# Weights decoded inside their own tile, one scaling of the first output weights, bounds in bfloat16, the next tile's input split in mid-tile, and due times from a backward schedule

## The chip, the cores and the metric

One core of one Trainium2 chip. The metric is the device time of one execution in microseconds (us). Of the core's engines this kernel uses TensorE (PE, matrix products; PEld is its weight load), VectorE (DVE), ScalarE (ACT), SyncE (SP, which here only issues DMA transfers) and, at the start, GpSimd (POOL). Each engine works through its own instructions in the order in which they were issued.

## The reference

```
out_up    = repeat(softmax(q_d k_d^T / 8) v_d, 4)          # q_d, k_d, v_d: means over 4 positions
out_local = softmax(mask(q k^T / 8, |i - j| < 4)) v
x  = (out_up + out_local) as 2304 tokens x 512             # 4 batches x 576, 8 heads x 64
h1 = x @ w1_in       (512 x 2048);  g1 = max(h1, 0) + log1p(exp(-|h1|));  y = g1 @ w1_out  (2048 x 512)
h2 = y @ w2_in       (512 x 2048);  g2 = h2 * cos(h2);                    z = g2 @ w2_out  (2048 x 512)
```

The weights arrive as float64, seen by the kernel as pairs of 32-bit integers, and are turned into float32 on the chip. A float32 product is made of three float16 products: each operand is scaled by a power of two and split into a high and a low float16, and high times high, high times low and low times high are added up in PSUM.

## The kernel before

**Tiles.** The 2304 tokens are four tiles of 512 and one of 256 (tile 4). The 2048 hidden features are 16 blocks f of 128. A unit is one (layer, tile, f): 12 matmuls of 512 columns make h (L884 and L897, PSUM ring h of two slots), ScalarE and VectorE turn it into g, high and low (L905 to L917 in layer 1, L930 to L945 in layer 2, then L966 and L970), and 12 matmuls add g's share to the layer's output (L974 and L989 in layer 1, L1016 and L1031 in layer 2), six for each of two accumulators, called half-units here. The output half lags its input half by LAG = 4 units.

**Weights.** A weight matrix is 8 blocks b of two f, 1 MB each as float64. L440 loads a block into one of two slots stg; ScalarE rebases the upper words into a float tile x (L453, a ring of three), VectorE shifts it (L458, join1, through the helper's L339) and puts in the lower words (L461, join2); ScalarE takes the sum of magnitudes as a bound (L467), and its elementwise output, which nobody reads, goes to the place of the block's final weights. From join2 on stg is free again; x is held until the block's low part is made. The bounds go through a transposing float32 matmul, the spread (L378, into a slot of ring h), and a maximum over columns (L385) to every partition; small VectorE steps make a power of two of it; then come the high part (L497) on ScalarE (L354) or VectorE (L356) and the low part on VectorE (L350). W1I, the first input weights, is scaled block by block; W1O, the first output weights, in four groups of two blocks, each with a scale of its own.

**Stages.** Four pairs of heads of the attention come first (12 more are put between units at fixed steps, POS1 to POS3), then layer 1 on tile 0 while W1I and W1O are decoded, then the other tiles, during which W2I and W2O are decoded, then layer 2. In tile 0 of layer 1 the four groups of W1O close their accumulators after every four f, and L1011 adds groups 1 to 3 to the output in float32. A tile's input must be scaled and split before its first unit: bounds per 128 features, a spread (ident_s by am), then high, low and a copy (L850, L378, L855 with L866 and tile xs). In layer 2 this is written at f = 0 of the tile itself (y_in, L1127); before tile 4 the backlog of output halves is drained to none (drain(0)).

**Order.** Every piece of work is an operation of a plan with a cost for each engine that may take it. `due` walks the operations from the last to the first and gives each the latest time at which it may end; only TensorE is taken there as something that does one thing at a time. `order` then lists the operations by due time, picks the engine where there is a choice, and puts fillers, matmuls of zeros (L1195), where TensorE would wait in the first 350 us of the plan. The order so found is pinned for every engine, and so are the filler matmuls.

## Time and profile before

| | us |
|---|---|
| median of 3 runs | 947.76 (947.12 to 948.87) |
| profiled execution, its own time | 947.95 |
| its span in the profile | 946.2 |
| TensorE busy | 899.2 (95%) |
| VectorE busy | 690.4 (73%) |
| ScalarE busy | 470.0 (50%) |

Busy TensorE is not all needed work: it includes the filler matmuls. The mean granted clock of TensorE was 0.986 of full speed; the two levels are 1.2 and 2.4 GHz, so that 0.50 in a row means the lower of them. In the timelines one row stands for several matmuls in a row on one line; the end of a matmul is modelled, and the distance of starts is the better measure of a unit.

### The profile page before, as it was taken

How to read it: one execution, taken by the hardware profiler on the slowest of the kernel's cores; microseconds unless marked ns; L12 is line 12 of the kernel's file. 1: busy time of each engine (PE TensorE's matmuls, PEld its weight loads, DVE VectorE, ACT ScalarE, POOL GpSimd, SP SyncE). 2: the span in 40 equal slices, each digit the busy share in tenths (PEclk: the TensorE clock that was granted, in tenths of full speed). 3: DMA queues.
4: the chain of work that ended last, by engine and by line, in shares of the span. 5: the costliest groups of instructions: out<-in, count | busy, mean ns of one | idle time of the engine just before them, and what ended most of it. 6: DMA issues, size and time to landing. Idle time of an engine off the chain costs nothing.

```text
span 946.2 us, 14558 instructions
## 1 busy us (share of the span) xinstructions
PE 899.2 (95%) x5809; PEld 469.7 (50%) x5809; DVE 690.4 (73%) x1474; ACT 470.0 (50%) x823; POOL 1.6 (0%) x11
## 2 busy tenths in 40 slices
PE   7899887799999999999999999999999999999797
PEld 4555443345555554444446864444444444444364
DVE  7999999976668776999964566567557656755465
ACT  3464696525445467879866632234224323422243
POOL 0000000000000000000000000000000000000000
PEclk9999998899999999999999999999999999999899
DMA  9557332400122003442200000010001000100100
GB/s 312 164 168 243 119 128 89 171 26 27 31 64 104 1 1 118 152 175 89 90 1 1 1 2 0 1 42 4 1 1 45 1 1 1 45 1 1 44 1 23
DMA packets 13363, 58.89 MB, mean 62 GB/s; under 512 B 1520, under 2 KB 1648, under 8 KB 9200
## 3 DMA queue, kind: packets, MB, share of 16 engines
q1 hardware_dynamic: 13296, 57.97, 17.7%
q8 instruction: 45, 0.74, 0.3%
q14 instruction: 22, 0.18, 0.1%
HBM read 53.25 MB, written 4.72 MB: 61 GB/s over the span
## 4 chain that ended last, share of the span: by engine, by line
PE 74%; DVE 16%; ACT 6%; DMA 2%; issue 1%; SPq 0%; ACTq 0%; DVEq 0%
PE h L897 34%; PE any L1031 19%; PE any L989 17%; DVE td L350 1%; DVE x L461 1%; PE any L724 1%; DVE sm L342 1%; DVE w1i_t L350 1%; DMA vd<-vd 1%; ACT ta L905 1%; DVE xt L350 1%; DMA qk<-qk 1%; DVE rs L602 1%; PE any L675 1%; DVE g L342 1%
## 5 line engine op out<-in xcount | busy, mean ns | idle before, releaser
L897 PE MATMUL h<-xt,w2i_t 128*128 128x512 f16 (+1 forms) x960 | 201.5, 362 | 9.5 <-DVE xt L866 5.3
L897 PE MATMUL h<-xt,w1i_t 128*128 128x512 f16 (+1 forms) x960 | 199.4, 360 | 9.3 <-DVE red L385 6.6
L1031 PE MATMUL any<-w2o_t,g 128*128 128x512 f16 x864 | 197.1, 379 | 0.3 <-DVE g L362 0.3
L989 PE MATMUL any<-g,w1o_t 128*128 128x512 f16 (+1 forms) x864 | 179.5, 357 | 2.3 <-ACT ed L646 1.4
L897 PEld LDWEIGHTS <-w2i_t 128*128 128x128 f16 x960 | 95.3, 99 | 105.7 <-issue 11.5
L897 PEld LDWEIGHTS <-w1i_t 128*128 128x128 f16 x960 | 93.8, 98 | 102.6 <-issue 14.2
L989 PEld LDWEIGHTS <-w1o_t 128*128 128x128 f16 x960 | 93.7, 98 | 89.1 <-issue 4.8
L930 ACT ACTIVATE ta<-h,quarter,i 128x512 f32<-128x512 f32 (+1 forms) x80 | 58.8, 735 | 155.2 <-PE h L897 155.2
L1031 PEld LDWEIGHTS <-g 128*128 128x128 f16 x864 | 84.5, 98 | 100.6 <-DVE g L362 0.8
L342 DVE TENSOR_TENSOR g<-td,g 128x512 f16<-128x512 f32 (+1 forms) x152 | 96.3, 634 | 8.0 <-ACT g L360 1.3
L905 ACT ACTIVATE ta<-h,i 128x512 f32<-128x512 f32 (+1 forms) x80 | 51.4, 642 | 80.7 <-PE h L897 67.4
L935 DVE TENSOR_SCALAR tb<-ta 128x512 f32<-128x512 f32 (+1 forms) x80 | 32.0, 400 | 77.6 <-ACT ta L930 77.1
L945 DVE SCALAR_TENSOR_TENSOR td<-h,r,tc 128x512 f32<-128x512 f32 (+1 forms) x80 | 55.8, 697 | 42.9 <-ACT tc L941 41.2
L941 ACT ACTIVATE tc<-ta 128x512 f32<-128x512 f32 (+1 forms) x80 | 46.9, 586 | 74.5 <-DVE ta L342 74.5
L350 DVE SCALAR_TENSOR_TENSOR td<-ta,sg,tb 128x512 f32<-128x512 f32 (+1 forms) x64 | 43.7, 682 | 48.4 <-ACT ta L917 48.0
L917 ACT ACTIVATE ta<-ta,one 128x512 f32<-128x512 f32 (+1 forms) x80 | 54.2, 680 | 2.0
L362 DVE CAST g<-td 128x512 f16<-128x512 f32 (+1 forms) x124 | 49.4, 398 | 8.0 <-PE any L989 0.8
L342 DVE TENSOR_TENSOR ta<-ta,tb 128x512 f32<-128x512 f32 (+1 forms) x80 | 51.0, 638 | 2.4
L909 ACT ACTIVATE tb<-h,r 128x512 f32<-128x512 f32 (+1 forms) x80 | 51.1, 639 | 0.0
L913 ACT ACTIVATE ta<-ta 128x512 f32<-128x512 f32 (+1 forms) x80 | 46.9, 588 | 0.0
L453 ACT ACTIVATE x<-stg 128x1024 f32<-128x1024 f32 x32 | 36.8, 1149 | 14.1 <-DVE w2i_t L350 3.8
L1195 PE MATMUL h<-zero 128*128 128x512 f16 x133 | 34.4, 393 | 5.3 <-POOL zero L1186 2.4
(147 smaller groups left out, 848.8 us busy)
## 6 DMA issues: line engine op xcount, KB each, us to landing
qk<-qk SPq DMA_DIRECT2D x16, 589.0 KB, 6.6
stg<-w1i SPq DMA_DIRECT2D x8, 1024.0 KB, 7.0
stg<-w1o SPq DMA_DIRECT2D x8, 1024.0 KB, 6.4
stg<-w2i SPq DMA_DIRECT2D x8, 1024.0 KB, 4.8
stg<-w2o SPq DMA_DIRECT2D x8, 1024.0 KB, 4.8
vw<-vw SPq DMA_DIRECT2D x16, 320.0 KB, 4.3
vd<-vd SPq DMA_DIRECT2D x16, 288.0 KB
out<-osb SPq DMA_DIRECT2D x18, 256.0 KB, 2.1
```

The costliest lines, as they stand in the source:

```text
L342: eng[e].tensor_tensor(out=out, in0=in0, in1=in1, op=op)
L350: nc.vector.scalar_tensor_tensor(out=out, in0=raw, scalar=s, in1=other, op0=ALU.mult, op1=op)
L362: nc.vector.tensor_copy(out, in_)
L897: nc.tensor.matmul(h.t[:, 0:n], l, r, start=(i == 0), stop=(i == 11))
L905: act(n, 1, True), lambda: nc.scalar.activation(out=a(), in_=h.t[:, 0:n], func=AF.Abs, scale=col(o.i1, f)),
L909: act(n, 1, True), lambda: nc.scalar.activation(out=b(), in_=h.t[:, 0:n], func=AF.Relu, scale=col(o.r1, f)),
L913: act(n), lambda: nc.scalar.activation(out=a(), in_=a(), func=AF.Exp, scale=-1.0),
L917: act(n, 1), lambda: nc.scalar.activation(out=a(), in_=a(), func=AF.Ln, bias=one),
L930: act(n, 2, True), lambda: nc.scalar.activation(out=a(), in_=h.t[:, 0:n], func=AF.Identity, scale=col(o.i2, f), bias=quarter), [h, *sc], [ ...
L945: dve(n, False, 1), lambda: nc.vector.scalar_tensor_tensor(out=td.t[:, 0:n], in0=h.t[:, 0:n], scalar=col(o.r1, f), in1=r(), op0=ALU.mult, ...
L989: nc.tensor.matmul(a.t[:, i, 0:n], l, r, start=(first and j == 0), stop=(last and j == 2))
L1031: nc.tensor.matmul(a.t[:, i], l, r, start=(f == 0 and j == 0), stop=(f == NF - 1 and j == 2))
```

## The change

- **In place.** A weight matrix is one flat tile of 17 half-blocks of 1024. The floats of block b lie where low(b) and high(b + 1) will stand. The ring x is gone; high(b) can be written only after low(b - 1) was made. The bound's unread output goes into stg, so a slot stg is held until the bound instead of until join2.
- **Groups.** W1I is decoded and scaled in two groups of four blocks. All of W1O is decoded from f = 10 of tile 0 on, its bounds are taken in two groups of four, and one set of steps scales all 16 columns together; layer 1 on tile 0 then has one accumulation over 16 f, as the other tiles have. W2 is scaled by pairs of blocks.
- **bfloat16 bounds.** The bounds of weights and inputs, and the matrix of ones-on-the-diagonal by which they are spread, are bfloat16.
- **Mid-tile.** In layer 2 the next tile's input is written into the plan at f = 8 of the tile before it, and tile 4 starts with four units still in the backlog.
- **Engines fixed.** For the first two batches of heads the copies C0, C1, D1 and up are on ScalarE alone, and so are the high parts of W1, of tile 0's and of tile 1's input, and a small step B1a of the attention.
- **Plan.** `due` schedules backward with VectorE and ScalarE, too, doing one thing at a time. The positions of four head pairs (POS1) and some costs of TensorE operations are changed.

```
 
 LAG = 4
-POS1 = (2, 5, 8, 11)
+POS1 = (6, 10, 15, 20)
 POS2 = (33, 37, 41, 45)
 POS3 = (50, 55, 60, 65)
 LAT = {"pe": 0.2, "act": 0.145, "dve": 0.13, "pool": 0.06, "sp": 0.95}
-NQK, NVD, NVW, NSM, NXB, NST, NGS = 3, 2, 3, 3, 3, 2, 8
+NQK, NVD, NVW, NSM, NST, NGS = 3, 2, 3, 3, 2, 8
-W2STEP = 1
+W2STEP = 2
+W2G = 2
+QKP, VP = (), ()
+YIN = 8
+DR4 = 4
+A_W, A_C, A_X, A_G = True, True, True, False
+CAP = ("pe", "dve", "act")
+OUT0 = 10
+IN0 = ((0, 4), (4, 4))
...
+        pre = {op: [] for op in self.ops}
+        for op in self.ops:
+            for x in op.succ:
+                pre[x].append(op)
...
+        while n:
+            best = None
+            cand = list(ready)
+            if pes and not left[pes[-1]]:
+                cand.append(pes[-1])
+            for op in cand:
+                for e in op.cost:
+                    x = (min(free[e], end[op]) if e in CAP else end[op], op.n)
+                    if best is None or x > best[0]:
+                        best = (x, op, e)
+            (x, _), op, e = best
+            if op is (pes[-1] if pes else None):
+                pes.pop()
+            else:
+                ready.remove(op)
+            op.due = x - op.cost[e]
+            if e in CAP:
+                free[e] = op.due
+            n -= 1
+            for q in pre[op]:
+                end[q] = min(end[q], op.due - LAT[min(q.cost, key=lambda z: q.cost[z])])
+                left[q] -= 1
+                if not left[q] and "pe" not in q.cost:
+                    ready.append(q)
 
         first = {}
         for op in self.ops:
...
 
-                raw, x = STG_.new(), XB_.new()
+                raw, x = STG_.new(), ("float", self.name, b)
...
                 def bound():
-                    nc.scalar.activation(
-                        out=self.t[:, 2 * b : 2 * b + 2, 0, :].bitcast(BF16), in_=x.t, func=AF.Abs,
-                        accum_out=self.bd[:, b : b + 1],
...
+                            out=out.rearrange("p (m e) -> p m e", m=2), in_=self.floats(b), func=AF.Abs,
+                            accum_out=self.bd[:, b : b + 1],
+                        )
+
+                P.add(act(1024), rebase, [raw], [x], [], nm + " rebase")
                 P.add(dve(1024, True), join1, [], [x], name=nm + " join1")
                 P.add(dve(1024), join2, [raw], [x], name=nm + " join2")
-                P.add(act(1024, 1), bound, [x], [("bd", self.name, b), *self.keys(b)], name=nm + " bound")
-                return x
+                P.add(act(1024, 1), bound, [x], [("bd", self.name, b), raw], name=nm + " bound")
...
-            def split(self, b, x):
-                w, s = lambda: self.t[:, 2 * b : 2 * b + 2], self.s[:, 2 * b : 2 * b + 1]
-                k = ("s", self.name, b)
+            def split(self, b):
+                s = self.s[:, 2 * b : 2 * b + 1]
+                x, k = ("float", self.name, b), ("s", self.name, b)
                 nm = f"{self.name}{b}"
+                over = [("float", self.name, b - 1)] if b else []
                 P.add(
-                    {**act(1024, 1), **dve(1024, True, 1)}, lambda e: scaled(e, w()[:, :, 0, :], x.t, s),
-                    [x, k], self.keys(b), name=nm + " high",
+                    either(act(1024, 1), dve(1024, True, 1), self.first and A_W), lambda e: scaled(e, self.his(b), self.floats(b), s),
+                    [x, k], self.keys(b) + over, name=nm + " high",
                 )
                 P.add(
-                    dve(1024, False, 1), lambda: less("dve", w()[:, :, 1, :], x.t, s, w()[:, :, 0, :]),
-                    [x, k], self.keys(b), name=nm + " low",
+                    dve(1024, False, 1), lambda: less("dve", self.los(b), self.floats(b), s, self.his(b)),
+                    [k], self.keys(b) + [x], name=nm + " low",
                 )
 
         W1I, W1O, W2I, W2O = Weight("w1i", w1i), Weight("w1o", w1o), Weight("w2i", w2i), Weight("w2o", w2o)
         W1I.place(wp)
         W1O.place(wp)
-        STG_, XB_ = STG, XB
+        STG_ = STG
+        raw0 = [dp.tile([128, 512], F32, name=f"raw{c}") for c in range(NC_)]
 
 
...
 
-        def group_scale(g):
+        def first_scale():
+
             o = T[0]
-            q = slice(4 * g, 4 * g + 4)
             return [
-                lambda: nc.vector.tensor_tensor(out=gs, in0=bits(o.lc[:, q]), in1=bits(W1O.s[:, q]), op=ALU.add),
-                lambda: nc.vector.tensor_reduce(col(kg, g), gs, axis=AX.X, op=ALU.min),
-                lambda: ts(bits(col(o.ikg, g)), col(kg, g), -1.0, ALU.mult, 381.0 * T23, ALU.add),
-                lambda: ts(bits(W1O.s[:, q]), bits(o.lc[:, q]), -1.0, ALU.mult, col(kg, g), ALU.add),
+                lambda: nc.vector.tensor_tensor(out=gs, in0=bits(o.lc), in1=bits(W1O.s), op=ALU.add),
+                lambda: nc.vector.tensor_reduce(o.k, gs, axis=AX.X, op=ALU.min),
+                lambda: ts(bits(o.ik), o.k, -1.0, ALU.mult, 381.0 * T23, ALU.add),
+                lambda: ts(bits(W1O.s), bits(o.lc), -1.0, ALU.mult, o.k, ALU.add),
             ]
 
...
-        def grp_in(b):
-            x = W1I.decode(b)
-            then = in_scale(0, 2 * b, 2, W1I, 14) + relu_scale(0, 2 * b, 2, T[0].lc)
-            W1I.scale(b, 1, then, [("sx", 0)], [("sc0", b)])
-            W1I.split(b, x)
-
-        def grp_out(g):
-            xs = [W1O.decode(2 * g), W1O.decode(2 * g + 1)]
+        def grp_in(b, n):
+            for i in range(n):
+                W1I.decode(b + i)
+            W1I.scale(b, n)
+            for i in range(n):
+                W1I.split(b + i)
+            then = in_scale(0, 2 * b, 2 * n, W1I, 14) + relu_scale(0, 2 * b, 2 * n, T[0].lc)
+            steps(
+                then, [("s", "w1i", b + i) for i in range(n)] + [("sx", 0), ("c", 0)],
+                [("sc0", b + i) for i in range(n)], "wthen",
+            )
+
+        def grp_out():
+            for b in range(NB):
+                W1O.decode(b)
+            W1O.scale(0, 4)
+            first = [("sc0", b) for b in range(NB)]
             W1O.scale(
-                2 * g, 2, group_scale(g), [("sc0", 2 * g), ("sc0", 2 * g + 1)],
-                [("sc0g", g)] + [("s", "w1o", 2 * g), ("s", "w1o", 2 * g + 1)],
+                4, 4, first_scale(), first + [("s", "w1o", b) for b in range(4)],
+                [("sc", 0)] + [("s", "w1o", b) for b in range(NB)],
             )
...
         for f in range(NF):
-            if f % 2 == 0:
-                grp_in(f // 2)
+            if f // 2 in dict(IN0) and f % 2 == 0:
+                grp_in(f // 2, dict(IN0)[f // 2])
+            if f == OUT0:
+                grp_out()
             unit_in(1, 0, f)
             step()
-        for g in range(4):
-            grp_out(g)
         for f in range(NF):
             l2(0, f)
             step()
...
             for _ in range(min(n, len(todo))):
                 W, b = todo.pop(0)
-                x = W.decode(b, after=[P.wrote["place2"]])
-                W.scale(b, 1)
-                W.split(b, x)
+                W.decode(b, after=[P.wrote["place2"]])
+                if b % W2G == W2G - 1:
+                    W.scale(b - W2G + 1, W2G)
+                    for a in range(b - W2G + 1, b + 1):
+                        W.split(a)
 
         for i, (k, t, f) in enumerate(seq):
             if f == 0:
...
         for i, (k, t, f) in enumerate(seq2):
-            if f == 0:
-                if t == 4:
-                    drain(0)
+            if i == 0:
                 y_in(t)
+            if f == YIN and t < 4:
+                y_in(t + 1)
+            if t == 4 and f == 0:
+                drain(DR4)
```

Three places in the order of instructions, first VectorE where the first output weights (w1o) get their scale. s_w1o holds the scales, lc those of the relu, gs, kg and ikg (now gs, k_0 and ik_0) the steps between; td, ta, tb and xt2 or xt3 belong to tile 0's activations, xt1 and xs0 to the input of tile 1, and x0 and x2 are slots of the ring x. Before, a group of two blocks (4 columns):

```order
L385 TENSOR_REDUCE red_1795<-h0_90 128x2
L350 SCALAR_TENSOR_TENSOR td0_96<-ta0_92,lc_0_159,tb0_94 128x512
L339 TENSOR_SCALAR s_w1o_150<-red_1795 128x4
L362 CAST xt2_84<-td0_96 128x512
L339 TENSOR_SCALAR s_w1o_150<-s_w1o_150 128x4
L342 TENSOR_TENSOR xt2_84<-td0_96,xt2_84 128x512
L810 TENSOR_TENSOR gs_219<-lc_0_159,s_w1o_150 128x4
L350 SCALAR_TENSOR_TENSOR td0_96<-ta1_93,lc_0_159,tb1_95 128x512
L811 TENSOR_REDUCE kg_218<-gs_219 128x1
L350 SCALAR_TENSOR_TENSOR xt1_83<-xt1_83,sx_1_179,xs0_97 128x512
L339 TENSOR_SCALAR ikg_217<-kg_218 128x1
L342 TENSOR_TENSOR xt2_84<-td0_96,xt2_84 128x512
L339 TENSOR_SCALAR s_w1o_150<-lc_0_159,kg_218 128x4
L866 COPY xt1_83<-xs0_97 128x512
L356 TENSOR_SCALAR w1o_t_156<-x0_106,s_w1o_150 128x2x512
L356 TENSOR_SCALAR xs0_97<-xt1_83,sx_1_179 128x512
L350 SCALAR_TENSOR_TENSOR w1o_t_156<-x0_106,s_w1o_150,w1o_t_156 128x2x512
L350 SCALAR_TENSOR_TENSOR w1o_t_156<-x2_108,s_w1o_150,w1o_t_156 128x2x512
```

Now, all 16 columns:

```order
L896 TENSOR_TENSOR gs_218<-lc_0_160,s_w1o_147 128x16
L391 SCALAR_TENSOR_TENSOR td0_96<-ta1_93,lc_0_160,tb1_95 128x512
L897 TENSOR_REDUCE k_0_166<-gs_218 128x1
L403 CAST xt3_85<-td0_96 128x512
L380 TENSOR_SCALAR ik_0_167<-k_0_166 128x1
L383 TENSOR_TENSOR xt3_85<-td0_96,xt3_85 128x512
L380 TENSOR_SCALAR s_w1o_147<-lc_0_160,k_0_166 128x16
L391 SCALAR_TENSOR_TENSOR td0_96<-ta0_92,lc_0_160,tb0_94 128x512
L919 TENSOR_REDUCE am1_1_236<-xm_1_181 128x1
L383 TENSOR_TENSOR qt0_116<-qk2_110 128x288 x2
L403 CAST xt3_85<-td0_96 128x512
L391 SCALAR_TENSOR_TENSOR w1o_t_153<-w1o_t_153,s_w1o_147 128x1024
L383 TENSOR_TENSOR xt3_85<-td0_96,xt3_85 128x512
L383 TENSOR_TENSOR qd0_117<-qt0_116 64x144 x2
L383 TENSOR_TENSOR qd0_117<-qt0_116 128x144
L391 SCALAR_TENSOR_TENSOR td0_96<-ta1_93,lc_0_160,tb1_95 128x512
L391 SCALAR_TENSOR_TENSOR w1o_t_153<-w1o_t_153,s_w1o_147 128x1024
```

The steps of four groups became one set; high parts (L356 before) no longer stand on VectorE, and between one low part (L391 STT on w1o_t) and the next other work was put.

Second, ScalarE during the decoding of w1o: the rebase is L453 before and L508 now, the bound L467 and L524. Before:

```order
L917 ACTIVATE ta1_93<-ta1_93,one_80 128x512
L453 ACTIVATE x0_106<-stg1_110 128x1024
L453 ACTIVATE x1_107<-stg0_109 128x1024
L467 ACTIVATE w1o_t_156,bd_w1o_149<-x0_106 128x2x512
L467 ACTIVATE w1o_t_156,bd_w1o_149<-x1_107 128x2x512
L905 ACTIVATE ta0_92<-h0_90,i1_0_157 128x512
L909 ACTIVATE tb0_94<-h0_90,r1_0_161 128x512
```

Now:

```order
L508 ACTIVATE w1o_t_153<-stg0_106 128x1024
L401 ACTIVATE aTd0_128<-any2_89 72x576
L999 ACTIVATE ta0_92<-ta0_92 128x512
L685 ACTIVATE sm1_123<-sm1_123 128x640
L728 ACTIVATE nd_2_229<-nd_2_229 96x3
L1003 ACTIVATE ta0_92<-ta0_92,one_80 128x512
L508 ACTIVATE w1o_t_153<-stg1_107 128x1024
L991 ACTIVATE ta1_93<-h1_91,i1_0_158 128x512
L995 ACTIVATE tb1_95<-h1_91,r1_0_162 128x512
L524 ACTIVATE stg0_106,bd_w1o_146<-w1o_t_153 128x1024
L401 ACTIVATE up0_129<-any0_87 128x144
L734 ACTIVATE ed0_125,sd_2_233<-any1_88,nd_2_229 96x144 x3
L524 ACTIVATE stg1_107,bd_w1o_146<-w1o_t_153 128x1024
```

The rebase of the second slot now stands ahead of the bound of the first, and the bound writes stg.

Third, TensorE where layer 2 goes from tile 3 to tile 4; am2_4 is tile 4's bound, xt4 its input, g the hidden activations. Before (the six last rows of the drain's matmuls, the spread, the first unit):

```order
L1031 LDWEIGHTS g7_105
L1031 MATMUL any1_88<-w2o_t_3386,g7_105 128x512
L1031 LDWEIGHTS g7_105
L1031 MATMUL any1_88<-w2o_t_3386,g7_105 128x512
L1031 LDWEIGHTS g7_105
L1031 MATMUL any1_88<-w2o_t_3386,g7_105 128x512
L378 MATMUL h1_91<-ident_s_77,am2_4_245 128x128
L897 LDWEIGHTS w2i_t_3385
L897 MATMUL h0_90<-xt4_86,w2i_t_3385 128x256
```

Now:

```order
L1109 MATMUL any1_88<-w2o_t_3252,g3_101 128x512
L1109 LDWEIGHTS g3_101
L1109 MATMUL any1_88<-w2o_t_3252,g3_101 128x512
L1109 LDWEIGHTS g3_101
L1109 MATMUL any1_88<-w2o_t_3252,g3_101 128x512
L419 LDWEIGHTS am2_4_244
L419 MATMUL h1_91<-ident_s_77,am2_4_244 128x128
L1109 LDWEIGHTS g4_102
L1109 MATMUL any2_89<-w2o_t_3252,g4_102 128x512
```

The spread of tile 4 moved from the end of tile 3's last output half to a place between two output halves.

## Rows read from the trace of the kernel before

**Rows 1.** The page: span, then busy time of each engine (share, instructions).
```profile
span 946.2 us, 14558 instructions
PE 899.2 (95%) x5809; PEld 469.7 (50%) x5809; DVE 690.4 (73%) x1474; ACT 470.0 (50%) x823; POOL 1.6 (0%) x11
```
**Rows 2.** Stretches: start:end, length, busy us (instructions) per engine, PEclk, DMA share, GB/s.
```profile
0.00:172.00 172.00, 143.83 (x1498) 83.24 (x1499) 162.50 (x383) 104.72 (x205) 1.64 (x11) 0.97 0.51 169
172.00:218.00 46.00, 43.96 (x202) 19.99 (x201) 35.41 (x76) 16.39 (x25) 0.00 (x0) 0.95 0.27 98
218.00:887.00 669.00, 663.88 (x3819) 336.22 (x3818) 457.42 (x918) 328.25 (x550) 0.00 (x0) 1.00 0.10 35
887.00:905.00 18.00, 11.25 (x55) 6.96 (x54) 10.44 (x36) 5.67 (x12) 0.00 (x0) 0.72 0.16 59
```
**Rows 3.** Timeline of TensorE in layer 2: start, us, line, shapes, count, [idle <- releaser].
```profile
588.73 2.75 PE L897 MATMUL h<-xt,w2i_t 128*128 128x512 f16 x12
591.32 2.75 PE L1031 MATMUL any<-w2o_t,g 128*128 128x512 f16 x12
```
**Rows 4.** Timeline of TensorE where tile 4 of layer 2 begins.
```profile
887.89 0.39 PE L378 MATMUL h<-ident_s,am 128*128 128x128 f32 x2
891.53 0.49 PE L897 MATMUL h<-xt,w2i_t 128*128 128x256 f16 x3 [3.25 <-DVE xt L866]
...
900.29 2.72 PE L897 MATMUL h<-xt,w2i_t 128*128 128x256 f16 x12 [1.48 <-DVE td L945]
902.80 1.74 PE L1031 MATMUL any<-w2o_t,g 128*128 128x512 f16 x6
904.38 2.85 PE L897 MATMUL h<-xt,w2i_t 128*128 128x256 f16 x24
```
**Rows 5.** Timeline of TensorE where tile 1 of layer 2 begins.
```profile
641.83 5.34 PE L897 MATMUL h<-xt,w2i_t 128*128 128x512 f16 x24 [0.92 <-DVE td L945]
```
**Rows 6.** Timeline of TensorE at tile 1 of layer 1.
```profile
218.40 2.75 PE L897 MATMUL h<-xt,w1i_t 128*128 128x512 f16 x12
```
**Rows 7.** Uses of tile xs up to 218: ns min/median/max, first and last start.
```profile
L866 DVE COPY xt<-xs x4: 285/287/289, 152.6 to 171.3; 128x512 f16<-128x512 f16 x4
```
**Rows 8.** VectorE by line and shape, 0 to 200: busy us, mean ns, idle before.
```profile
L461 DVE SCALAR_TENSOR_TENSOR x<-stg,x 128x1024 int32<-128x1024 int32 x16 | 19.3, 1214 | 0.0
...
L339 DVE TENSOR_SCALAR x<-x 128x1024 int32<-128x1024 int32 x16 | 10.9, 685 | 1.2 <-ACT x L453 1.2
...
L350 DVE SCALAR_TENSOR_TENSOR w1i_t<-x,s_w1i,w1i_t 128x1024 f16<-128x1024 f32 x8 | 10.2, 1279 | 0.1
```
**Rows 9.** ScalarE by line and shape, 0 to 200.
```profile
L453 ACT ACTIVATE x<-stg 128x1024 f32<-128x1024 f32 x16 | 18.3, 1143 | 9.6 <-DVE w1o_t L350 3.8 <-DMA stg<-w1i 3.7 <-DVE w1i_t L350 2.0
...
L917 ACT ACTIVATE ta<-ta,one 128x512 f32<-128x512 f32 x16 | 11.5, 726 | 0.2
...
L467 ACT ACTIVATE w1o_t<-x 128x1024 bf16<-128x1024 f32 x7 | 7.4, 1053 | 3.9 <-DVE x L461 3.9
L354 ACT ACTIVATE w1i_t<-x,s_w1i 128x1024 f16<-128x1024 f32 x5 | 5.8, 1155 | 1.0 <-DVE s_w1i L339 1.0
```
**Rows 10.** Stretch 0 to 40, columns as in rows 2.
```profile
0.00:40.00 40.00, 32.15 (x394) 19.37 (x394) 33.44 (x85) 14.48 (x35) 1.64 (x11) 1.00 0.81 273
```
**Rows 11.** The page's DMA issues: KB each, median us to landing.
```profile
stg<-w1i SPq DMA_DIRECT2D x8, 1024.0 KB, 7.0
```
**Rows 12.** Timeline of SyncE's queue, issues of weight blocks.
```profile
75.11 0.33 SPq L440 DMA_DIRECT2D stg<-w1i  x1
...
85.14 0.33 SPq L440 DMA_DIRECT2D stg<-w1i  x1
```
**Rows 13.** Timeline of TensorE around the first output weights.
```profile
148.33 9.94 PE L897 MATMUL h<-xt,w1i_t 128*128 128x512 f16 x36 [5.00 <-DVE red L385]
```
**Rows 14.** Stretch in which those matmuls began, columns as in rows 2.
```profile
146.00:152.00 6.00, 3.67 (x9) 1.32 (x9) 6.00 (x15) 4.30 (x9) 0.00 (x0) 0.50 0.94 350
```
**Rows 15.** TensorE by line and shape, whole program: filler matmuls on ring h.
```profile
L1195 PE MATMUL h<-zero 128*128 128x512 f16 x133 | 34.4, 393 | 5.3 <-POOL zero L1186 2.4 <-ACT tb L909 1.6 <-ACT ed L646 1.1
```

More of the change, by code (lines that the diff above doesn't have):

```diff
@@ L172, in cool @@
                 return False
+            cost = min(cost, 2.4)
             a0 = now + cost - WIN
@@ L554, in sum4, with sums, place @@
                 two(e, vs.t, tv.t[:, :, 0], tv.t[:, :, 1], ALU.add)
-            aop({"dve": 0.74}, sum1, [tk], [qt], [qt, qd], nm + "sum1")
-            aop({"dve": 0.66}, sum2, [qt], [qd], [], nm + "sum2")
+            pa, sm = BANK.new(), SM.new()
+            if b in QKP:
+                hs = (HB if b == 0 else BANK).new()
+                hst = lambda: hs.t if b == 0 else hs.t[:, 0]
+                def sums():
+                    x = tk.t[:, :, 3 : 3 + S].rearrange("p a (i r) -> p a i r", r=4)
+                    for a in range(2):
+                        for r in range(4):
+                            nc.tensor.matmul(
+                                hst()[:, SD * a : SD * a + SD], ident, x[:, a, :, r], start=(r == 0), stop=(r == 3)
+                            )
+                def place():
+                    for j in range(2):
+                        h = slice(64 * j, 64 * j + 64)
+                        copy("act", qd.t[h, SD * j : SD * j + SD], hst()[h, 0:SD])
+                    nc.scalar.activation(
+                        out=qd.t[:, 2 * SD : 3 * SD], in_=hst()[:, SD : 2 * SD], func=AF.Copy, scale=float(2.0**-7)
+                    )
+                aop(pe(2.3), sums, [tk, "ident"], [hs], [hs], "sums " + nm)
+                aop({"act": 0.85}, place, [hs], [qd], [qd], nm + "place")
+            else:
+                aop({"dve": 0.74}, sum1, [tk], [qt], [qt, qd], nm + "sum1")
+                aop({"dve": 0.66}, sum2, [qt], [qd], [], nm + "sum2")
+            nmx, r = carr_small("nm", NG * 2), carr_small("rs", NG * 2)
             if b == 0:
```

171 lines of the change are left out of this document (87 added, 84 removed).

## Prediction

> **What bounds the kernel now.** I read the page first: TensorE is busy for 899.2 of 946.2 us [rows 1], so no other engine can bound the program as a whole, and time is lost where TensorE waits or multiplies zeros. The stretches show where that is. From 218 to 887 it is busy for 663.9 of 669 us at full clock [rows 2]; the change can take little there. Two places remain. From 0 to 172 TensorE is busy for 143.8 us, fillers among it (133 of them on ring h alone [rows 15]), and VectorE for 162.5 of 172 [rows 2]: that first stage belongs to VectorE. From 887 to 905 TensorE is busy for 11.3 of 18 us at 0.72 of its clock [rows 2]: that is the start of tile 4 in layer 2. So I make two sums, A for layer 2 and B for the first stage.
>
> **A, the next tile's input in mid-tile.** The price of TensorE's work: 12 matmuls of 512 columns take 2.59 us from start to start, 588.73 to 591.32 [rows 3], so 0.216 for one, 0.108 for one of 256 columns, and 1.295 for a half-unit of six. Where tile 4 begins, the spread ends at 888.28 and steady work starts at 904.38. Between them lie 36 matmuls of 256 columns and 6 of 512, worth 5.2 us. The other 10.9 us are waiting for the input's split (3.25 at first) and for the first unit's activations (1.48), and the low clock [rows 4, 2]. At tile 1 only 0.92 us is lost [rows 5], for four output halves in the backlog cover the rest; I count that three times, 2.7 in all. In the new order the spread of tile 4 stands between two output halves of tile 3, and the split has half a tile of TensorE's time, over 40 us, to be done in: both losses go, -13.6.
>
> What the move costs: the spread takes a slot of ring h in mid-tile, four times, so that two units in a row share the other slot. Nothing in the trace shows that. It is bounded by zero, for the output halves may cover it, and by the 0.92 of [rows 5], a wait for the same chain of activations. I take about the middle, 0.5 each, +2.0. The splits' VectorE work is moved, not added, and VectorE has 211 us to spare between 218 and 887 [rows 2]. **A = -11.6.**
>
> **B, the first stage.** My landmark is the first matmul of layer 1 on tile 1. It stands at 218.40 now [rows 6], although its input's last copy started at 171.3 [rows 7]: after that TensorE had the output matmuls of tile 0 to do, 43.96 of 46 us [rows 2]. In the new order it stands in the middle of these matmuls, and waits for that same copy. So I ask when VectorE gets there, and how much of TensorE's work is then left.
>
> VectorE's work up to that copy, counted in the two orders. More: three blocks more to join (16 for 13) at 1.21 + 0.69, so +5.7, and six low parts more (16 for 10) at 1.28, +7.7 [rows 8]. Less: attention steps (177 for 206 instructions), high parts and input high parts (none for 9), small steps (38 for 58) and reductions (6 for 11). The 63 that go are worth, at 0.2 to 0.4 us each (VectorE's mean here is 162.5 us over 383, 0.42 [rows 2], and short steps pull it down), 13 to 25 us. So VectorE's work is the same or up to 12 us less; I take the same, 162.5 us, since most of what goes is short. The four groups' extra additions of L1011 lie behind the copy and no longer matter.
>
> VectorE's idle time was 9.5 us of 172 [rows 2], of which 6.6 at the very start [rows 10], while the first loads land; that stays. New are two waits. One is the staging: a slot now takes a landing of 7.0 [rows 11], a rebase of 1.14, joins of 0.69 and 1.21 and a bound of 1.05 [rows 8, 9], 11.1 us at least, and two slots serve 16 blocks in 8 rounds. The issues at 75.11 and 85.14, one slot's turn with the other slot's issue between them, are 10 us apart [rows 12], so such rounds occur. The first issue is at some 10 us and the last bound must be done at about 138 for the rest of the order to fit behind it, so there are 16 us for a round, and queue waits of up to 4.9 fit in. I let VectorE stand for 1.1 us a round, 9 in all; the bounds are 1.2, the idle time that the rebase ends now [rows 8], and 39 if all 4.9 fell on it. The other is the chain in W1O: each high part, 1.16 on ScalarE [rows 9], waits for the low part before it, and each low part for its high part. Ahead of a high part may stand an activation of 0.73 [rows 9], so up to 1.9 for each of eight blocks, 15 us; the order has other VectorE work between two low parts, so at least 0. I take 3.5, nearer to zero for that reason. Idle time 6.6 + 9 + 3.5 = 19, and the copy is done at 162.5 + 19 = 181.5.
>
> TensorE at that point: by the order 15 of the 32 half-units of tile 0's output stand behind the landmark, 19.4 us that lay ahead of it before; a few small products of the attention more and cheaper spreads are about even. The 17 ahead of it, 22 us, need the first low part of W1O at about 159, which is where VectorE's sum stands there.
>
> The clock: after a wait of 5.00 us, 36 matmuls took 9.94 us, and 7.77 by the steady price [rows 13]; the granted clock was 0.50, the lower level, in that stretch [rows 14]. The output of tile 0 now starts after one longer wait for W1O, so +2.2. **B** = 181.5 + 19.4 + 2.2 - 218.4 = **-15.3**.
>
> Of the other parts: scaling W2 by pairs and decoding it in place lies beside a TensorE that is 99% busy [rows 2], at zero; if that cover failed it would show as waits of the first units of layer 2 for w2i, at most one round, 11 us. The new due times have no price of their own; what they do is in the order that I counted from.
>
> The Trainium skill ("SBUF — State Buffer", section "The DMA setup-cost knee") says that a transfer of 1 MiB lands at about 330 to 340 GB/s, an estimate of 3.1 us for a block. By that the rounds would be almost 4 us shorter, the staging stalls would vanish and the time would be about 912. Here other loads run beside them, the trace has 7.0 us [rows 11], and the measurement decides.
>
> **Sum.** 946.2 - 11.6 - 15.3 = 919.3 of span; the profiled execution took 947.95, 1.75 more than its span, and 0.2 more than the median of the runs, which I leave out. So 921.
>
> **Rivals.**
> 1. Staging turns against it, slower. The slot is held through the bound, and in ScalarE's order the next slot's rebase stands ahead of that bound, so a late join blocks both slots. Every microsecond on a round moves the landmark by 8. The gain of 26.9 is gone at 3.4 us more, a round of 19.4; at 20.5 the time is 921 + 36 = 957. For it: the ring of three x that decoupled the joins is gone, and ScalarE already sat 9.6 us ahead of the rebases [rows 9]. Against it: at 16 the round has 4.9 us over its parts.
> 2. The first stage gains nothing: high and low parts take turns at full price (+11.5) and staging takes some 4 us more. A alone is left: 936.
> 3. The split in mid-tile doesn't do what it says, because VectorE comes to it only late in the tile; A is zero: 932.6. Against it: VectorE is busy for 457 of 669 us there [rows 2].
> 4. The clock. There are 140 filler matmuls for 205. If each of some five waits of the first stage that had fillers now ends at the lower level, at 2.2 each [rows 13], the time is 932. The Trainium skill ("TensorE: Matmul & The Clock Gate", section "What's actually happening") speaks for it: the default state is throttled, and activity releases it. The trace agrees as far as [rows 14] goes. Against it: the fillers are placed in the new plan by the same rule, and the mean clock was 0.97 up to 172 [rows 2].
>
> **How the numbers follow.** Chances: forecast 0.56, rival 2 0.20, rival 1 0.12, rival 4 0.07, rival 3 0.05. The range: with idle time as before (9.5 less), no clock cost and no cost in ring h it would be 907; at the top it takes in rivals 2 to 4. So 906 to 938; above it lies rival 1, and parts of the others. What measurement can tell from no change here is about 0.2%, 1.9 us. Faster by more than that are the forecast and rivals 2 to 4 nearly whole, 0.87; rival 1 gives 0.10 to slower and, with the thin end of rival 2, 0.03 to no difference.
>
> **What would show it.** The first matmul of layer 1 on tile 1 at about 200 or before, within 4 us of the end of VectorE's copy of tile 1's input, with 15 half-units behind it; VectorE's idle time up to there near 19 us; slot rounds of 16 us by the issues of weight blocks; and at the start of tile 4 no wait of TensorE over 1 us and a granted clock of 1.00. I would be wrong if TensorE waits for W1O beyond 165, if VectorE's waits for ScalarE's rebases come to over 30 us, or if waits in layer 2 at ring h exceed 1 us per tile.

## The result and the profile after

The changed kernel took 903.11 us (median of 4 runs, 901.8 to 904.3) against 947.81 in the same batch: a ratio of 0.9527, 95% interval 0.9511 to 0.9544. That is 44.7 us less where 26.9 were forecast, and lies below the range of 906 to 938. The direction was right and the two places were right; the sizes were too small. The profiled execution has a span of 900.0 us, 46.2 less than before; it was the fastest of its four (901.8), so spans and landmarks that are compared with it below mostly show 1 to 2 us more than the medians do.

The page of the changed kernel, first the lines that answer to [rows 1]:

```profile
span 900.0 us, 14222 instructions
PE 869.6 (97%) x5702; PEld 452.8 (50%) x5702; DVE 659.1 (73%) x1352; ACT 480.4 (53%) x861; POOL 1.6 (0%) x11
...
PEclk9999999999999999999999999999999999999999
```

The granted clock no longer has a slice under 0.9. Stretches, columns as in [rows 2]:

```profile
0.00:170.40 170.40, 145.55 (x1462) 81.24 (x1462) 161.26 (x332) 126.66 (x240) 1.64 (x11) 0.99 0.55 187
140.00:172.00 32.00, 29.20 (x136) 13.04 (x134) 31.83 (x63) 21.39 (x30) 0.00 (x0) 1.00 0.14 43
600.00:860.00 260.00, 260.00 (x1249) 121.94 (x1248) 166.41 (x332) 86.28 (x132) 0.00 (x0) 1.00 0.04 13
```

170.40 is the landmark of the prediction, the first matmul of layer 1 on tile 1 (218.40 before, [rows 6]). Up to it VectorE works for 161.3 us, 1.2 less than in the 172 us of [rows 2], and is idle for 9.1. From 600 to 860 in layer 2 TensorE does not wait at all. The same in the timelines of TensorE, first around the landmark (L1074 is the output half of layer 1, L983 the input half, L419 a spread):

```profile
145.92 2.75 PE L1074 MATMUL any<-g,w1o_t 128*128 128x512 f16 x12
148.67 0.22 PE L419 MATMUL h<-ident_s,am 128*128 128x128 bf16 x1
148.73 7.93 PE L1074 MATMUL any<-g,w1o_t 128*128 128x512 f16 x36
156.49 10.52 PE L1074 MATMUL any<-xt,w1o_t 128*128 128x512 f16 x48
169.11 1.46 PE L1074 MATMUL any<-g,w1o_t 128*128 128x512 f16 x6 [2.09 <-DVE sm L383]
170.40 2.75 PE L983 MATMUL h<-xt,w1i_t 128*128 128x512 f16 x12
```

The outputs of tile 0 begin at 145.92 and run at full clock; 102 matmuls, 17 half-units, stand ahead of the landmark as counted. TensorE's only wait among them, 2.09 us, ends with a step of the attention on VectorE (sm, which reads a slot of the ring any); the landmark itself follows without a wait. Before, TensorE had fillers and waits from 159 on, and the outputs began at 173.70:

```profile
159.68 5.99 PE L1195 MATMUL h<-zero 128*128 128x512 f16 x27 [0.96 <-ACT tb L909]
...
171.49 0.79 PE L378 MATMUL h<-ident_s,bd_w1o 128*128 128x128 f32 x2 [5.61 <-ACT w1o_t L467]
173.70 14.46 PE L989 MATMUL any<-g,w1o_t 128*128 128x512 f16 x60 [1.42 <-ACT ed L646]
```

Then at the start of tile 4, which answers to [rows 4]:

```profile
840.64 2.75 PE L1109 MATMUL any<-w2o_t,g 128*128 128x512 f16 x12
843.24 2.78 PE L983 MATMUL h<-xt,w2i_t 128*128 128x256 f16 x24
845.86 2.75 PE L1109 MATMUL any<-w2o_t,g 128*128 128x512 f16 x12
```

No idle time, every distance is the steady 2.6 us. What VectorE waited for up to the landmark (us in all, times, longest):

```profile
DVE qt L383 <- DMA qk<-qk: 3.9, 1, 3.9
DVE w1i_t L391 <- ACT w1i_t L395: 1.2, 2, 0.6
DVE w1o_t L380 <- ACT w1o_t L508: 0.9, 1, 0.9
```

The third row is the staging (join1 waits for a rebase): 0.9 us where I had put 9. The second is the chain of high and low parts in W1I, 1.2; in W1O, where I had put 3.5, it is 0.2. The loads, issues on SyncE's queue by start:

```profile
39.26 1.60 SPq L495 DMA_DIRECT2D stg<-w1i  x2
...
50.33 3.81 SPq L495 DMA_DIRECT2D stg<-w1i  x2
...
61.36 6.06 SPq L495 DMA_DIRECT2D stg<-w1i  x2
...
75.35 2.69 SPq L495 DMA_DIRECT2D stg<-w1o  x2
...
86.59 0.33 SPq L495 DMA_DIRECT2D stg<-w1o  x1
...
90.59 0.33 SPq L495 DMA_DIRECT2D stg<-w1o  x1
...
101.17 2.62 SPq L495 DMA_DIRECT2D stg<-w1o  x2
...
113.62 3.66 SPq L495 DMA_DIRECT2D stg<-w1o  x2
```

After a first round of 27.5 us the rounds take 11.0 to 14.6, not the 16 of the forecast. The landings on the page (KB each, median us), for [rows 11]:

```profile
stg<-w1i SPq DMA_DIRECT2D x8, 1024.0 KB, 6.0
stg<-w1o SPq DMA_DIRECT2D x8, 1024.0 KB, 5.0
```

### The profile page after: what moved, and what is told of

The parts are those of the page before. It is cut to its first block, busy times and chain, and to the rows that moved or that the text cites. A ratio compares the mean times of both kernels' runs of the same rounds, so it can differ in the third digit from the quotient of the medians.

```text
span 900.0 us, 14222 instructions
## 1 busy us (share of the span) xinstructions
PE 869.6 (97%) x5702; PEld 452.8 (50%) x5702; DVE 659.1 (73%) x1352; ACT 480.4 (53%) x861; POOL 1.6 (0%) x11
## 4 chain that ended last, share of the span: by engine, by line
PE 75%; DVE 13%; ACT 7%; DMA 3%; issue 1%; SPq 0%; DVEq 0%; ACTq 0%
PE h L983 35%; PE any L1109 21%; PE any L1074 16%; ACT stg L524 1%; DVE sm L383 1%; DMA stg<-w2o 1%; PE any L815 1%; DVE w1o_t L391 1%; DVE td L391 1%; ACT ta L991 1%; DMA stg<-w1o 1%; DVE nm L679 1%; DVE qd L383 1%; ACT tb L995 1%; PE any L716 1%
## 5 line engine op out<-in xcount | busy, mean ns | idle before, releaser
L983 PE MATMUL h<-xt,w1i_t 128*128 128x512 f16 (+1 forms) x960 | 199.5, 360 | 7.5 <-ACT tb L995 3.5
L983 PE MATMUL h<-xt,w2i_t 128*128 128x512 f16 (+1 forms) x960 | 199.0, 358 | 0.0
L1074 PE MATMUL any<-g,w1o_t 128*128 128x512 f16 (+1 forms) x864 | 177.9, 355 | 2.3 <-DVE sm L383 2.1
L983 PEld LDWEIGHTS <-w1i_t 128*128 128x128 f16 x960 | 93.4, 98 | 101.0 <-issue 8.1
L983 PEld LDWEIGHTS <-w2i_t 128*128 128x128 f16 x960 | 93.9, 98 | 94.9
L1074 PEld LDWEIGHTS <-w1o_t 128*128 128x128 f16 x960 | 92.8, 98 | 88.8 <-issue 3.6
L391 DVE SCALAR_TENSOR_TENSOR td<-ta,sg,tb 128x512 f32<-128x512 f32 (+1 forms) x64 | 43.6, 681 | 49.4 <-ACT ta L1003 48.9
L1285 PE MATMUL h<-zero 128*128 128x512 f16 x105 | 27.7, 397 | 3.4 <-POOL zero L1276 2.4
L395 ACT ACTIVATE xs<-xt,sx 128x512 f16<-128x512 f32 (+1 forms) x27 | 18.3, 679 | 20.7 <-DVE xt L952 14.4
```

What stands on the lines that cost most here:

```text
L391: nc.vector.scalar_tensor_tensor(out=out, in0=raw, scalar=s, in1=other, op0=ALU.mult, op1=op)
L983: nc.tensor.matmul(h.t[:, 0:n], l, r, start=(i == 0), stop=(i == 11))
L1074: nc.tensor.matmul(a.t[:, i, 0:n], l, r, start=(first and j == 0), stop=(last and j == 2))
```

## The experiments

Fifteen runs, each beside the kernel before on the same chip; the ratio is to that, with its 95% interval (the changed kernel has 0.9527). "Landmark" is the first matmul of layer 1 on tile 1. Three kinds: parts undone, with a new order by the planner; the same order with one cost changed; one part alone in the kernel before.

| run | median us | ratio | landmark |
|---|---|---|---|
| W1O in four groups again | 928.4 | 0.9771 (0.9724 to 0.9819) | 218.1 |
| input split at the tile's start again | 919.9 | 0.9704 (0.9682 to 0.9727) | 175.8 |
| W1O written at f = 15 | 915.0 | 0.9641 (0.9626 to 0.9655) | 171.5 |
| the same, W1I block by block | 923.4 | 0.9733 (0.9717 to 0.9750) | 206.5 |
| engines free | 908.7 | 0.9581 (0.9563 to 0.9599) | 198.7 |
| due times of before | 905.1 | 0.9548 (0.9517 to 0.9579) | 174.8 |
| slot free from join2, planned so | 914.7 | 0.9638 (0.9601 to 0.9674) | 199.4 |
| same order: float32 bounds | 906.7 | 0.9568 (0.9541 to 0.9594) | 172.4 |
| same order: bound's output elsewhere | 900.3 | 0.9487 (0.9467 to 0.9508) | 169.4 |
| same order: no fillers | 905.2 | 0.9548 (0.9516 to 0.9580) | 175.6 |
| same order: 480 KB more per block | 908.9 | 0.9585 (0.9541 to 0.9630) | 178.6 |
| same order: bound taken twice | 918.3 | 0.9668 (0.9647 to 0.9690) | 187.8 |
| same order: every load twice | 970.7 | 1.0244 (1.0214 to 1.0274) | 241.6 |
| before: split in mid-tile alone | 934.4 | 0.9862 (0.9834 to 0.9890) | 218.7 |
| before: new due times alone | 950.0 | 1.0008 (0.9988 to 1.0027) | 219.1 |

A landmark that moves need not move the end, since a plan may do more of tile 0's outputs ahead of it (engines free: 198.7, but only 5.6 us more). Only between runs of the same order it stands for time. What the parts undone cost is not to be added up either, since each got an order of its own. No run undoes the decoding in place, the pairs of W2's blocks or the new positions of the attention; what these are worth alone is not shown.

**Layer 2.** The split put back to the tile's start:

```diff
-            if i == 0:
-                y_in(t)
-            if f == YIN and t < 4:
-                y_in(t + 1)
-            if t == 4 and f == 0:
-                drain(DR4)
+            if f == 0:
+                if t == 4:
+                    drain(0)
+                y_in(t)
```

> The changed kernel (903.1 us) with one part undone: in layer 2 the next tile's input is written at f = 0 of the tile itself again, and tile 4 starts with an empty backlog. Theory: the input split at the tile's start costs what the kernel before lost there, 10.9 us at tile 4 and 0.9 at each of tiles 1 to 3, so 13.6 more: 916.7, with TensorE waiting for xt at tile 4 and a granted clock under 0.8 there. Forecast's own sum: 11.6 more, 914.7. Rival, that the extra gain lies in layer 2: more than 17 us more, over 920.

919.9, 16.8 more. The loss at tile 4 is back, in rows that copy [rows 4]:

```profile
866.79 0.49 PE L983 MATMUL h<-xt,w2i_t 128*128 128x256 f16 x3 [3.42 <-DVE xt L952]
...
875.57 2.72 PE L983 MATMUL h<-xt,w2i_t 128*128 128x256 f16 x12 [1.48 <-DVE td L1031]
```

That is above the 13.6 expected. The profiled execution has a span 21.2 us longer: from the first unit of layer 2 to the end it takes 394.3 us for 379.5, 14.8 more, and the rest lies ahead, where the first unit of tile 0 starts 6 us later in the new order (64.2 for 58.4). The reverse, in the kernel before:

```diff
-            if f == 0:
-                if t == 4:
-                    drain(0)
+            if i == 0:
                 y_in(t)
+            if f == 8 and t < 4:
+                y_in(t + 1)
+            if t == 4 and f == 0:
+                drain(4)
```

> The kernel before with one part alone: the next tile's input of layer 2 at f = 8 of the tile before, tile 4 started with four units in the backlog. Theory 1: all of the loss at the tiles' starts goes, 13.6 or a little more: 933 to 934.5, no wait of TensorE over 0.5 us in layer 2. Forecast: 11.6 less, 936, with waits of about 0.5 us in mid-tile for ring h. Rival 3: no gain, 947.

934.4, 13.9 less (1.38%, interval 1.10 to 1.66%). Theory 1 holds; at tile 4 TensorE goes through without a wait:

```profile
872.15 2.75 PE L1031 MATMUL any<-w2o_t,g 128*128 128x512 f16 x12
874.74 2.78 PE L897 MATMUL h<-xt,w2i_t 128*128 128x256 f16 x24
```

From the first unit of layer 2 to the end this run takes 389.3 us for 404.2. So A is 13.9 by the medians and 14.9 by the profile, and not 11.6: nothing is paid for the slot of ring h in mid-tile, and the waits that go were 1.3 more than the 13.6 that I had counted.

**The output weights.** W1O in four groups of two blocks, with their accumulators and additions, as the functions of before have it:

```diff
-            if f == OUT0:
-                grp_out()
+            if f == OUT0:
+                for g in range(4):
+                    grp_out(g)
```

> The changed kernel with W1O in four groups of two blocks again, each with its scale, its accumulators and its additions of L1011 (emitted at f = 10 as now). Theory 1: scaling all at once saves VectorE the three further sets of steps and six additions of 1.28 us, about 10 us of work on the engine that sets the first stage, half of it ahead of tile 1's input: 907 to 913. Theory 2: a first group ready early lets TensorE begin the outputs of tile 0 sooner, which is worth as much: 900 to 904.

928.4, 25.3 more, two and a half times what theory 1 allowed; theory 2 falls, as the outputs of tile 0 begin at 156.27 instead of 145.92. VectorE's additions (L1099) account for much of the size, columns as in the other timelines:

```profile
183.22 2.58 DVE L1099 SCALAR_TENSOR_TENSOR xt<-any,ikg,xt 128x1024 f32<-128x1024 f32 x2 [5.16 <-PE any L1077]
193.58 2.58 DVE L1099 SCALAR_TENSOR_TENSOR xt<-any,ikg,xt 128x1024 f32<-128x1024 f32 x2 [7.78 <-PE any L1077]
203.94 1.28 DVE L1099 SCALAR_TENSOR_TENSOR xt<-any,ikg,xt 128x1024 f32<-128x1024 f32 x1 [7.78 <-PE any L1077]
```

The order puts tile 1's last copies behind these additions (they start at 210.1 to 217.1), so VectorE stands for 20.7 us while TensorE works off the groups, and then, from 206 to 218, TensorE has little but fillers and waits. Of the parts undone this one costs most. When W1O is written into the plan matters too:

```diff
-OUT0 = 10
+OUT0 = 15
```

> The changed kernel with W1O written into the plan at f = 15 of tile 0 instead of f = 10 (control for the next run). The order goes by due times, so little is expected: 901 to 907.

915.0, 11.9 more, outside what was expected. The landmark is nearly where it was, but the outputs of tile 0 start late, and TensorE fills the gap:

```profile
150.42 4.69 PE L1285 MATMUL h<-zero 128*128 128x512 f16 x21 [1.30 <-ACT tb L995]
159.52 12.17 PE L1074 MATMUL any<-g,w1o_t 128*128 128x512 f16 x42 [4.41 <-DVE sm L383]
```

42 matmuls took 12.17 us there, the lower clock in the first of them (granted 0.50 from 159.5 to 165); the changed kernel began its outputs at 145.92. So 7 half-units stand ahead of the landmark and not 17, and the other ten, 13 us of TensorE's work, are left for later, which fits the 11.9.

**The input weights,** block by block, on top of the last:

```diff
-IN0 = ((0, 4), (4, 4))
+IN0 = tuple((b, 1) for b in range(8))
```

> As the control, with W1I scaled block by block again (eight sets of steps instead of two). Theory 1: six sets of some eight short VectorE steps more, 6 x 8 x 0.17 = 8 us on the engine that sets the first stage: 6 to 9 more than the control. Theory 2: the first units of tile 0 begin earlier, which pays for the steps: within 3 of the control.

8.4 us over its control, the size of theory 1, but not its mechanism: VectorE's work in the whole program is 663.1 us for 660.9, 2.2 more and not 8. The outputs of tile 0 begin 9.2 us later (168.74 for 159.52), in another order. What causes that is open:

```profile
162.36 3.18 PE L1285 MATMUL h<-zero 128*128 128x512 f16 x14 [0.49 <-DVE red L426]
168.74 6.61 PE L1074 MATMUL any<-g,w1o_t 128*128 128x512 f16 x23 [3.20 <-ACT ed L734]
```

**Engines and due times.**

```diff
-A_W, A_C, A_X, A_G = True, True, True, False
+A_W, A_C, A_X, A_G = False, False, False, False
```

> The changed kernel with the choice of engine given back to the planner (attention copies C0, C1, D1, up, high parts of W1 and of the inputs of tiles 0 and 1). Theory 1: fixing them to ScalarE took about 6 us of work from VectorE, which sets the first stage: 5 to 8 us more, 908 to 911, VectorE busy for 165 us or more up to tile 1's input. Theory 2: the planner chose ScalarE for most of them anyway: 902 to 905.

908.7, 5.6 more: theory 1, and VectorE's work in the whole program is 665.6 us for 659.1, 6.5 more. The due times of before in the changed kernel, and the new ones in the kernel before (the core of the first; the second is its reverse):

```diff
-            op.due = x - op.cost[e]
-            if e in CAP:
-                free[e] = op.due
+            if "pe" in op.cost:
+                end = min(end, nxt)
+                nxt = end - cost
+            op.due = end - cost
```

> The changed kernel with the due times of the kernel before (only TensorE does one thing at a time in them); the parts and their operations are the same, the order is not. Theory 1: the backward schedule with capacities is what keeps VectorE supplied in the first stage; without it VectorE's idle time up to tile 1's input rises from 9 to 19 us or more, the first matmul of layer 1 on tile 1 moves from 170 to over 180, and the time is over 913. Theory 2: the grouping of the weights does it, and the due times matter little: 901 to 907, landmark at 168 to 174.

> The kernel before with the backward schedule with capacities alone (everything else as it was). Theory 1: the due times gave little in the changed kernel (2 us), so also here: 943 to 948. Theory 2: the old order is where the first stage lost its time, TensorE idle from 140 to 172: 920 to 938.

905.1 and 950.0; the first interval overlaps that of the changed kernel, and the second holds 1. So theory 2 of the first run holds (its landmark, 174.8, is just outside what was written), and of the second theory 1 in substance (its time is 2 us above what was written). No gain of the backward schedule can be told here, in either kernel.

**Bounds.** float32 for the six tiles of bounds and ident_s, same order.

```diff
-        ident_s = const.tile([128, 128], BF16, name="ident_s")
+        ident_s = const.tile([128, 128], F32, name="ident_s")
```

> The changed kernel, same order, with the bounds and the spread's matrix in float32 again. Behind the first matmul of tile 1 stand 24 spreads (16 for the second layer's weights, 8 for inputs). Theory 1: a float32 spread costs TensorE some 0.2 us more than a bfloat16 one, and behind that point TensorE has no idle time to hide it: 4 to 6 more, 907 to 909. Theory 2, spreads cost nothing that counts (as the prediction took them): 902 to 904.

906.7, 3.6 more, just under theory 1's lower bound; the intervals overlap by a hair. One group of spreads (partition and column sizes, type, count, busy us and mean ns), with float32, then in the changed kernel:

```profile
L419 PE MATMUL h<-ident_s,bd_w2i 128*128 128x128 f32 x16 | 2.4, 274 | 0.0
```

```profile
L419 PE MATMUL h<-ident_s,bd_w2i 128*128 128x128 bf16 x8 | 1.1, 219 | 0.0
```

Eight spreads are 16 matmuls with float32 and 8 with bfloat16.

**Clock.** No fillers, same order.

```diff
         for op in P.order():
+            if op.n < 0:
+                continue
```

> The changed kernel, same order, without its 140 filler matmuls. Theory 1, rival 4 of the prediction: after each of some five longer waits TensorE's work begins at the lower clock level, 2.2 us each, 11 more or over: 914 or more, mean granted clock under 0.98. Theory 2, VectorE sets the first stage and slower matmuls hide behind it: 901 to 906.

905.2: theory 2. The clock did fall, but next to VectorE that costs little. By the medians it is 2.1 us, within the intervals; in the profiled execution the landmark comes 5.2 us later and the span is 4.1 longer, so it isn't nothing:

```profile
40.00:100.00 60.00, 44.26 (x371) 26.47 (x373) 56.03 (x112) 47.47 (x86) 0.00 (x0) 0.72 0.69 240
```

**Staging.** First the slot freed at join2 as before, by another tile for the bound's output (the first two lines), then planned so (all four):

```diff
-                    out = raw.t.rearrange("p m e -> p (m e)")[:, 0:256].bitcast(BF16)
+                    out = dump
...
-                P.add(act(1024, 1), bound, [x], [("bd", self.name, b), raw], name=nm + " bound")
+                P.add(act(1024, 1), bound, [x], [("bd", self.name, b)], name=nm + " bound")
```

> The changed kernel, same order, but the bound's elementwise output goes to a tile of its own, so that a staging slot is free from join2 on, as before the change. Theory 1, staging is covered: rounds get shorter by up to 2 us, but VectorE waited only 0.9 us for rebases, so the time stays within 1.5 us of 903. Theory 2, holding the slot sets the pace (rival 1 in a mild form): each of 8 rounds gives 1 us or more, 895 or less.

> The changed kernel with the bound's output in a tile of its own, planned so that the slot is free from join2 on (the earlier run with that tile kept the order). Theory 1: VectorE's own work, 160 of 170 us, is the limit, and rounds that are 1 to 2 us shorter give little more than the 3 us of the earlier run: 897 to 902. Theory 2: staging is the limit: under 895.

900.3 with the same order: 2.8 less, more than theory 1's 1.5 and far from theory 2. It is the fastest of all these kernels; its interval lies below that of the changed kernel. In the changed kernel the slot is held past the end of join2 by 1.1 to 4.4 us for a block, the bound's 1.06 and its place in ScalarE's queue. The plan made for the freed slot took 914.7: VectorE's in-order queue then holds a bound of the outputs ahead of tile 1's last copies,

```profile
DVE xm L937 <- ACT xt L396: 19.1, 1, 19.1
```

so both theories of that run missed, and a new plan can cost more than the wait that it was to remove. Up to there it was ahead: the last bound of W1O ends at 118.2 instead of 128.6, and the outputs of tile 0 begin at 135.69 instead of 145.92. What a freed slot is worth in an order without that wait is open. Then longer rounds: loads doubled, 480 KB more in front of each, and the bound twice.

```diff
+                    for _ in range(2 if self.first else 1):
+                        nc.sync.dma_start(raw.t, self.dram[:, 2 * b : 2 * b + 2, :])
...
+                    if self.first:
+                        nc.sync.dma_start(extra[b % 2], self.dram[:, 2 * b, 0:480])
...
+                        for _ in range(2 if self.first else 1):
                             nc.scalar.activation(
```

> The changed kernel, same order, with every load of a block of the first layer's weights issued twice into its slot, so that a landing of 5 to 6 us becomes one of 8 to 10 us, 3 to 4 more per round of two slots. Theory 1, the rounds lie under other work of VectorE: the slack takes most of it, under 911. Theory 2, the rounds set the pace (the price of rival 1, 8 us for each us of a round): 24 to 32 more, 927 to 935, with VectorE waiting for rebases for over 20 us where it waited 0.9.

> The changed kernel, same order, with a load of 480 KB into a tile that nobody reads ahead of each 1 MB block of the first layer's weights: no wait of SyncE for the slot's own landing as in the doubled load, only less bandwidth, 1 to 1.5 us more for a landing, 2 to 3 for a round of two. Theory 1, rounds have some slack before VectorE waits: under 908. Theory 2, no slack (the doubled load gave 71 us for 8 rounds): 8 us for each us of a round, 915 to 927.

> The changed kernel, same order, with each bound of the first layer's weights taken twice: the slot is held 1.06 us longer for each block, on ScalarE alone, no load is touched (the mirror of the run that frees the slot 1 us earlier). Theory 1, rounds and VectorE's work are about in balance with some slack: 0 to 3 more, 903 to 906. Theory 2, each us of a round counts eightfold: 9 to 18 more, 912 to 921, with VectorE waiting for rebases for 8 us or more.

The doubled load cost 67.6 us and moved the landmark by 71. VectorE's waits up to 240 in it:

```profile
DVE w1o_t L380 <- ACT w1o_t L512: 24.9, 7, 4.9
DVE w1i_t L380 <- ACT w1i_t L512: 22.3, 5, 8.3
DVE raw L833 <- ACT up L401: 16.5, 2, 13.0
```

The first two are the staging, theory 2. So is the third in the main: these copies of the attention (up) stand behind rebases in ScalarE's queue, the longest behind two that waited 8.5 and 6.2 us for their landings. The attention's loads stood behind on SyncE's queue, too, but VectorE's waits for them are 4.9 us, for 4.6 in the changed kernel. Rounds after the first took 19.4 to 23.0 us, 8.4 more on average. The second load of a block was issued only when the first had landed, by these waits of SyncE:

```profile
SPq L496 <- DMA stg<-w1i: 53.5, 8, 10.2
SPq L496 <- DMA stg<-w1o: 44.5, 8, 7.4
```

The 480 KB cost 5.8 us, between the theories. The first unit of tile 0 starts 7 us later there (65.3 for 58.4), and VectorE waits only 3.6 us for rebases. The first round is 4.4 us longer, the six after it 3.5 in all. Up to 45 us ScalarE waits 6.2 us for the first two landings of weights (1.6 in the changed kernel), and a copy of the attention behind them keeps VectorE for 4.5, so more of the cost is the first landings than the rounds:

```profile
ACT w1i_t L514 <- DMA stg<-w1i: 6.2, 2, 3.6
...
DVE raw L835 <- ACT up L402: 4.5, 1, 4.5
```

The bound twice cost 15.2 us and moved the landmark by 17.4, theory 2 by its size but not by its mechanism. VectorE's longest waits up to the landmark there:

```profile
DVE w1i_t L391 <- ACT w1i_t L395: 5.1, 4, 1.9
DVE xt L830 <- ACT up L401: 3.7, 3, 2.2
DVE raw L830 <- ACT up L401: 3.6, 2, 2.6
...
DVE w1i_t L380 <- ACT w1i_t L508: 1.5, 2, 1.0
```

Rebases are a small part; what ScalarE hands to VectorE comes later as a whole. The run added 16 x 1.06 = 17 us to ScalarE's queue and the landmark moved by as much, while freeing the slot at join2 without touching ScalarE's work moved it by 1.0. ScalarE up to the landmark, columns as in [rows 2] (its busy time is the fourth):

```profile
0.00:187.80 187.80, 153.36 (x1461) 84.46 (x1462) 162.31 (x332) 143.86 (x272) 1.64 (x11) 0.95 0.50 169
```

It works 17.2 us more than in the changed kernel and is idle as long (43.9 us for 43.7), and its waits for landings of weights are 7.3 us for 5.8. That speaks for ScalarE's queue, and against the holding of the slot, as what the first stage has no slack in, in this order; the two are not told apart by a run that holds a slot longer and leaves ScalarE alone, which wasn't tried.

## Why the prediction was right and wrong

Right: that TensorE loses its time in two places; that the landmark would come to stand in the middle of tile 0's outputs, 1.2 us behind VectorE's last copy (169.0 to 169.3); that VectorE's work up to it stays the same (161.3 for 162.5 us); that 15 half-units stand behind it; and that fillers and clock are no rival of weight. Not as I had it: TensorE doesn't wait for that copy, its last wait ends one VectorE instruction ahead of it, and the outputs begin at 145.92 where I had them begin at about 159.

Wrong is the size, by 19.3 us of span (919.3 forecast, 900.0 measured). By the terms of the sum:

- **VectorE's idle time**, 19 forecast, 9.1 measured: 9.9. This is the step that failed; with the 1.2 of the next term it puts the last copy's end at 169.3 and not at 181.5. I let VectorE stand for 1.1 us in each of 8 rounds, 9 in all, and put 3.5 on the chain of high and low parts in W1O; the trace has 0.9 for the rebases and 1.4 for the chains, of which 0.2 in W1O. The rounds after the first took 11.0 to 14.6 us instead of 16. A landing took 5.0 to 6.0 us for the 7.0 of [rows 11], which is a part of that; the rest isn't taken apart by a run. In VectorE's order other work stood where I had it wait. I had the order in hand and guessed a flat stall per round instead of reading from it what stands between the joins.
- **VectorE's work**: 1.2 less.
- **The clock**, 2.2 forecast, none: the outputs of tile 0 now begin without a long wait, at 1.00 from 140 to 172.
- **Ring h in mid-tile**, 2.0 forecast, none, shown by 260.00 of 260 us and by the split alone in the kernel before.
- **The spreads.** What is left, 4.0, lies behind the landmark. I had called cheaper spreads "about even" with other small products. The profiled float32 run has a span of 904.9, 4.9 more than the changed kernel; its landmark is 2.0 later, so 2.9 of it lies behind. That is most of the 4.0. The last 1.1 fits the waits of layer 2: by the split alone they were 14.9 and not the 13.6 counted, 1.3 more.

The lower end of the range, 907, was the sum with idle time as before, no clock and no ring cost. Idle time, clock and ring h came out just so; the spreads, the waits of layer 2 and VectorE's slightly smaller work took it below. The range had the right ends for the terms that I doubted and none for one that I had set at zero.

Rivals: the slower one did not come to pass. Its price came out about right: with doubled loads, rounds 8.4 us longer on average moved the landmark by 71, some 8 for each us. Its condition, rounds of 19.4 us, did not occur in the changed kernel. By the Trainium skill ("SBUF — State Buffer", section "The DMA setup-cost knee") a block would land in about 3.1 us, an estimate; the trace has 5.0 to 6.0 now and 7.0 before, so the measurement stays above it, although its consequence, vanishing stalls, came true.

What the forecast had no price for is how much the grouping of W1O is worth by itself: I set the four groups' additions at nothing, as they lie behind the copy. In the order that the planner makes for groups in the new kernel they stand ahead of it, and undoing that one part, new order included, costs 25.3 us.

## What to carry to other kernels

Where one in-order engine is busy for 95% of a stage and a second one feeds it, the second can be on the path too, even at 74%: here 17 us of work added to it came out at the end nearly whole (15.2), while a staging slot freed earlier gave 1 to 3 us in the same order. Taking work from it wasn't tried. A stall that a moved wait may cause is read from what stands in the order between the producer and the waiting instruction, not set per round. And on an engine that bounds the rest of the program, small operations that get cheaper are counted to the last one, since nothing hides them.

## What the runs showed of the hardware

Weight blocks of 1 MB landed in 4.6 to 7.5 us in the changed kernel. The page's medians are 6.0 and 5.0 us in the first stage, where the attention's loads run beside them, and 4.8 later:

```profile
stg<-w2i SPq DMA_DIRECT2D x8, 1024.0 KB, 4.8
```

Without fillers TensorE's granted clock was 0.72 from 40 to 100 us, so that a part of the time was at the lower level, and the program took 2.1 us more by the medians and 4.1 by the spans. A spread of 128 x 128 shows as two records of 274 ns on TensorE with float32 and as one of 219 ns with bfloat16.
